# Batch 0 loaded in fp32 over two queues, local v in one transfer per head, and all local masks on Pool, in a sparse-attention and MLP kernel

## The chip, the cores and the metric

The kernel runs on 1 core of one Trainium2 chip. The metric is the device time of one execution in microseconds (us). One look at a kernel gives a profile and a time; where small differences matter it is run several times, in turn with the kernel before on the same chip.

## The reference, cut to what matters

```python
batch, n_heads, seq, head_dim = (8, 8, 576, 64)      # q, k, v: fp32
stride = 32
rel = pos[:, None] - pos[None, :]
mask_local   = (rel >= 0) & (rel < stride)                                  # heads 0..3
mask_strided = (rel >= 0) & (pos[None, :] % stride == pos[:, None] % stride)  # heads 4..7
x = softmax(where(mask, q @ k.T / 8, -1e9)) @ v      # then to [4608, 512]
h = x @ w_in                                         # w_in  [512, 2048]
out = (h * tanh(softplus(h))) @ w_out                # w_out [2048, 512], result fp32
```

## The kernel before

A head loads and computes the attention of batch 0. Then come nine blocks of the MLP, each of 512 tokens: `mlp1` (x to h), then `mlp2` (h to out). The attention of batch t+1 is cut into small steps, which are put between the groups of matmuls of block t. So blocks 0 to 6 carry attention, the last two are MLP alone. "Strided" tiles have 72 partitions, "local" ones 96 or 128.

Loads and casts. Strided k and q are cast from fp32 to bf16 by the transfer itself, which is issued by Pool (GpSimd); everything else of q, k and v comes as fp32 through SP and is cast by an engine. The fp32 buffers `vs32`, `vl32`, `kl32`, `ql32` exist once, so the loads for a later batch wait until the casts of the earlier one are done.

```python
    def load_qk_str(b):
        for dst, src in ((ks, k), (qs, q)):
            nc.gpsimd.dma_start(
                dst[b % 2][0:PN], src[b, 4:8].rearrange("h (p j) d -> p h (j d)", j=CS)
            )
    # ... load_qk_loc: the same for heads 0..3, on nc.sync, into kl32 and ql32 ...

    def load_v(b):
        nc.sync.dma_start(vs32[0:PN], v[b, 4:8].rearrange("h (p j) d -> p h j d", j=CS))
        nc.sync.dma_start(vl32[32:128, 0, :, :], v[b, 0:4, 0:96, :].rearrange("h p d -> p h d"))
        for i in range(1, NW):
            nc.sync.dma_start(
                vl32[:, i, :, :],
                v[b, 0:4, WQ * i - 32:WQ * i + WQ, :].rearrange("h p d -> p h d"),
            )
    # ...
    def cast_v(b, e_s, e_l):
        cast(e_s, vs[b % 2][0:PN, :, :, 0:D], vs32[0:PN])
        for i in range(0, NW, 3):
            cast(e_l, vl[b % 2][:, i:i + 3, :, 0:D], vl32[:, i:i + 3, :, :])
```

The steps of the attention inside a block: `Q` is scores, exponential and mask, with the engine of the mask as its last argument; `V` is P times v and the division by the row sum; `X` transposes to the layout of the MLP.

```python
        return [
            [Q("s", 0, Dv)], [], [Q("s", 1, Dv)],
            [Q("s", 2, Po), V("s", 0)],
            [Q("l", 0, Po), V("s", 1)],
            [Q("l", 1, Po), V("s", 2), V("s", 3)],
            [Q("l", 2, Dv), V("s", 4)], [V("s", 5), V("s", 6)],
            # ... the other V and X steps ...
        ]
```

The head and the main loop:

```python
        load_qk_str(0)
        # ... ident, stm ...
        load_qk_loc(0)
        # ... loc ...
        load_v(0)
        # ... memsets on Dv; transposes of strided k and q ...
        cast_qk_loc(0, Po, Dv)
        cast(Po, vs[0][0:PN, :, :, 0:D], vs32[0:PN])
        load_w_in(0, 2)
        # ... strided scores and masks (Dv); local v cast by Po; load_w_in(2, 4) ...
        # ... local scores and masks (Dv) ...
        for j in range(8):
            a.pv("s", j)
        # ...
        load_qk_loc(1)
        load_v(1)
        # ... the rest of the attention of batch 0 ...
        load_qk_str(1)
        for c in range(4):
            nc.gpsimd.dma_start(w_out[:, 4 * c:4 * c + 4, :], ...)
        cast_qk_loc(1, Po, Po)
        cast_v(1, Po, Po)
        load_qk_str(2)
        # ... load_qk_loc(2), load_v(2) ...
        for t in range(NBLK):
            gT, g1 = mlp1(t)
            # ... mlp1 groups with the transposes of batch t+1 between them ...
            if t + 3 < B:
                load_qk_str(t + 3)
            # ... mlp2 groups with the attention steps of batch t+1 between them ...
            # ... casts of batch t+2 on Po, loads of batch t+3 ...
```

The softmax here doesn't subtract the row's maximum and nothing guards it: scores larger than these inputs give would overflow.

Of the kernel before, what the change touches and what calls it, by code (L numbers as in the profile page):

```python
# [10 lines left out]
F32 = mybir.dt.float32  # L11
BF16 = mybir.dt.bfloat16
AF = mybir.ActivationFunctionType
# [3 lines left out]
NW = 6  # L17
WQ = 96
CL, PL = 6, 96
CS, PN = 8, 72  # L20
# [15 lines left out]
def kernel(ctx, tc, q, k, v, moe_w_in, moe_w_out, out):  # L36
    nc = tc.nc
    B, H, S, D = q.shape
# [8 lines left out]
    loc_h = nc.inline_tensor(loc_np, name="locmask")  # L47
    stm_h = nc.inline_tensor(stm_np, name="strmask")
    ident_h = nc.inline_tensor(
        np.eye(128, dtype=np.float32).astype(ml_dtypes.bfloat16), name="ident"  # L50
    )
# [45 lines left out]
# [5 lines that stand above are left out]
# [5 lines left out]
                src[b, 0:4].rearrange("h (p j) d -> p h (j d)", j=CL),  # L107
            )

    def load_v(b):  # L110
        nc.sync.dma_start(vs32[0:PN], v[b, 4:8].rearrange("h (p j) d -> p h j d", j=CS))
        nc.sync.dma_start(vl32[32:128, 0, :, :], v[b, 0:4, 0:96, :].rearrange("h p d -> p h d"))
        for i in range(1, NW):
            nc.sync.dma_start(
                vl32[:, i, :, :],
                v[b, 0:4, WQ * i - 32:WQ * i + WQ, :].rearrange("h p d -> p h d"),
            )

    def load_w_in(c0, c1):
        for c in range(c0, c1):  # L120
# [5 lines left out]
    def cast(eng, out_, in_):  # L126
        if eng is nc.scalar:
            nc.scalar.copy(out_, in_)  # L128
        else:
            eng.tensor_copy(out_, in_)  # L130

    def cast_qk_loc(b, e_k, e_q):
        for e, dst, src in ((e_k, kl, kl32), (e_q, ql, ql32)):
            cast(e, dst[b % 2][0:PL].rearrange("p j h d -> p h j d"), src[0:PL])
# [131 lines left out]
    def attn_steps(b):  # L266
        a = Attn(b)
        Po, Dv = nc.gpsimd, nc.vector
        Q = lambda kd, i, e: (lambda: a.qk(kd, i, e))
        V = lambda kd, i: (lambda: a.pv(kd, i))  # L270
        X = lambda kd, hf: (lambda: a.xt(kd, hf))
        return [
            [Q("s", 0, Dv)], [], [Q("s", 1, Dv)],
            [Q("s", 2, Po), V("s", 0)],
            [Q("l", 0, Po), V("s", 1)],
            [Q("l", 1, Po), V("s", 2), V("s", 3)],
            [Q("l", 2, Dv), V("s", 4)], [V("s", 5), V("s", 6)],
            [V("s", 7), V("l", 0)], [V("l", 1)], [X("s", 0), V("l", 2)],
            [X("s", 1), V("l", 3)], [X("l", 0), V("l", 4)], [V("l", 5)],
            [X("l", 1)], [],  # L280
        ]
# [48 lines left out]

    with tc.manual_schedule():
        Po, Dv, Sc = nc.gpsimd, nc.vector, nc.scalar
        load_qk_str(0)
        nc.sync.dma_start(ident[:], ident_h.ap())
        nc.sync.dma_start(stm[:], stm_h.ap())
        load_qk_loc(0)
        nc.sync.dma_start(loc[:], loc_h.ap())
        load_v(0)
        Sc.preload_act_table(AF.Exp)
        Dv.memset(kTs[:, 16 * PN:16 * PN + 64], 0.0)  # L340
        Dv.memset(kTl[:, :, 0:32], 0.0)
        Dv.memset(vl32[0:32, 0, :, :], 0.0)
# [3 lines left out]
        for i in range(2):  # L346
            Dv.memset(vl[i][0:32, 0, :, D:D + 1], 0.0)
        for p in P_s + P_l:
            Dv.memset(p[:], 0.0)

        a = Attn(0)
        t_step(0, "s", "k", 0, Dv)
        t_step(0, "s", "k", 1, Dv)
        t_step(0, "s", "q", 0, Sc)
        t_step(0, "s", "q", 1, Sc)
        cast_qk_loc(0, Po, Dv)
        cast(Po, vs[0][0:PN, :, :, 0:D], vs32[0:PN])
        load_w_in(0, 2)
        a.qk("s", 0, Dv)
# [5 lines left out]
        for hp in range(2):  # L365
            t_step(0, "l", "k", hp, Dv)
            t_step(0, "l", "q", hp, Sc)
        a.qk("l", 0, Dv)
        a.qk("l", 1, Dv, True)
        a.qk("l", 2, Dv, True)  # L370
        for j in range(8):
            a.pv("s", j)
        nc.sync.dma_start(gate[:], x_s[0:1, 5, :])
# [77 lines left out]
```

## Time and profile before

| | kernel before |
|---|---|
| median of 3 runs before the prediction | 355.98 us |
| median of the 4 runs beside the changed kernel | 356.06 us (355.93 to 356.62) |
| span of the profiled run, TensorE busy | 354.6 us, 318.3 us |
| first matmul of the MLP | 37.23 us |
| block 0: start of `mlp1(0)` to start of `mlp1(1)` | 37.23 to 75.19 = 37.96 us |
| blocks 1 and 2 | 36.47 and 36.46 us |

"Idle before" in square brackets is the time for which the engine did nothing ahead of that line, and the arrow names what ended it. The lines which the prediction rests on stand in it (timelines: start, duration, engine, line, operation). Two more views matter later. The first is the timeline of Pool in block 0 of the kernel before (start, duration, engine, line, operation):

```profile
53.66 0.83 POOL L130 CAST vl<-vl 128x768 bf16<-128x768 f32 x1 [3.18 <-DMA vl<-in_v_dram]
55.51 0.83 POOL L130 CAST vl<-vl 128x768 bf16<-128x768 f32 x1 [1.02 <-DMA vl<-in_v_dram]
...
60.34 1.27 POOL L211 TENSOR_TENSOR Ps<-Ps,stm 72x576 bf16<-72x576 bf16 x1 [1.19 <-ACT Ps L209]
```

Local v of batch 1 lands by 55.5 us, and the strided mask waits for its exponential on ScalarE, not the reverse: Pool is there in time, with 1.19 us to spare.

The second is the timeline of TensorE's weight loads at the start of the MLP. Each 128x512 matmul has one, so their spacing is the rate of the matmuls:

```profile
40.17 0.15 PEld L301 LDWEIGHTS <-w_in 128*128 128x128 bf16 x1 [0.28 <-issue]
40.60 6.63 PEld L301 LDWEIGHTS <-w_in 128*128 128x128 bf16 x31 [0.27 <-issue]
```

From 37.23 to 40.60 us one comes every 0.43 us; from there on every 0.214 us (6.63 us for 31). The MLP starts at half rate and loses about 1.7 us by it.

### The profile page before, as it was taken

The numbers are of one execution on the slowest core, as the hardware profiler recorded it, in microseconds if no ns is written. First come the engines' busy times: TensorE is split into PE (matmuls) and PEld (weight loads), VectorE is DVE, ScalarE is ACT, GpSimd is POOL, SyncE is SP. The second block draws the span as 40 slices with busy tenths as digits, with TensorE's granted clock in tenths as the row PEclk, the third lists the DMA queues.
The fourth block names the chain that finished last, engine by engine and source line by source line (L and its number), as shares of the span: only waits on it lengthen the run. The fifth ranks groups of instructions, "written<-read, shape, count | busy, mean of one in ns | idle before, by whom it ended". The sixth has DMA issues, their size and how long they took to land.

```text
span 354.6 us, 6492 instructions
## 1 busy us (share of the span) xinstructions
PE 318.3 (90%) x2784; PEld 171.2 (48%) x2784; DVE 124.9 (35%) x327; ACT 173.6 (49%) x190; POOL 100.6 (28%) x88
## 2 busy tenths in 40 slices
PE   0537999899989998999899989998999989999994
PEld 0424454455445544554469745554555454444441
DVE  3478025632363236323642364235613460000000
ACT  1431556275636564556446653666275636514611
POOL 3290236911091109310841065005600400000000
PEclk9999999999999999999999999999999999999999
DMA  7999999969611991099109901870110011011012
GB/s 172 187 163 211 265 187 213 179 167 233 108 61 59 217 139 59 20 246 148 48 15 238 172 4 61 207 139 1 61 61 0 3 61 59 0 61 59 0 44 76
DMA packets 49073, 39.03 MB, mean 110 GB/s; under 512 B 27284, under 2 KB 42132, under 8 KB 49044
## 3 DMA queue, kind: packets, MB, share of 16 engines
q1 hardware_dynamic: 38420, 29.70, 36.1%
q0 software_dynamic: 10624, 8.92, 16.2%
q8 instruction: 22, 0.36, 0.5%
q14 instruction: 7, 0.06, 0.1%
HBM read 38.08 MB, written 9.44 MB: 134 GB/s over the span
## 4 chain that ended last, share of the span: by engine, by line
PE 79%; DVE 8%; ACT 6%; DMA 3%; issue 3%; POOL 0%; ACTq 0%; POOLq 0%
PE psh L301 36%; PE pso L316 29%; PE po L227 4%; DMA qs<-in_q_dram 3%; PE tr L150 2%; PE tr L159 2%; ACT Pl L209 2%; DVE Pl L211 2%; PE ps L191 2%; ACT Ps L209 2%; DVE x_s L234 2%; PE ps L202 2%; DVE Ps L211 1%; DVE qTl L130 1%; PE trx L257 1%
## 5 line engine op out<-in xcount | busy, mean ns | idle before, releaser
L316 PE MATMUL pso<-w_out,gT 128*128 128x512 bf16 x576 | 141.5, 379 | 0.0
L301 PE MATMUL psh<-xT,w_in 128*128 128x512 bf16 (+1 forms) x640 | 135.3, 361 | 0.8 <-ACT xT L128 0.7
L305 ACT ACTIVATE gT<-psh 128x1024 bf16<-128x1024 f32 x72 | 73.8, 1024 | 55.9 <-PE psh L301 55.7
L301 PEld LDWEIGHTS <-w_in 128*128 128x128 bf16 x640 | 60.3, 99 | 55.3 <-issue 3.4
L316 PEld LDWEIGHTS <-gT 128*128 128x128 bf16 x576 | 49.0, 97 | 44.3
L128 ACT COPY xT<-trx 128x576 bf16<-128x576 bf16 x32 | 20.4, 639 | 55.4 <-PE trx L257 39.5
L211 POOL TENSOR_TENSOR Ps<-Ps,stm 72x576 bf16<-72x576 bf16 x7 | 8.9, 1269 | 101.4 <-ACT Ps L209 101.4
L323 ACT COPY osb<-pso 128x1024 f32<-128x1024 f32 x18 | 18.2, 1012 | 27.8 <-PE pso L316 27.8
L233 DVE RECIPROCAL rden<-po 72x4 f32<-72x4 f32 (+1 forms) x112 | 19.7, 176 | 29.6 <-PE po L227 29.6
L227 PE MATMUL po<-vs,Ps 72*128 72x65 bf16 x256 | 18.2, 201 | 11.8 <-DVE rden L233 8.7
L234 DVE TENSOR_TENSOR x_s<-po,rden 72x256 bf16<-72x256 f32 x64 | 26.9, 420 | 2.2
L209 ACT ACTIVATE Pl<-ps 128x768 bf16<-128x768 f32 x24 | 19.2, 811 | 13.8 <-PE ps L191 13.8
L130 DVE COPY kTs<-tr 128x576 bf16<-128x576 bf16 x16 | 7.3, 458 | 47.6 <-PE tr L150 47.5
L211 POOL TENSOR_TENSOR Pl<-Pl,loc 128x768 bf16<-128x768 bf16 x14 | 22.6, 1639 | 1.9 <-ACT Pl L209 1.9
L209 ACT ACTIVATE Ps<-ps 72x864 bf16<-72x864 f32 (+1 forms) x24 | 19.1, 806 | 7.1 <-PE ps L202 7.0
L211 DVE TENSOR_TENSOR Ps<-Ps,stm 72x864 bf16<-72x864 bf16 (+1 forms) x17 | 14.0, 831 | 23.5 <-ACT Ps L209 23.5
L227 PEld LDWEIGHTS <-Ps 72*128 72x128 bf16 x256 | 12.6, 101 | 18.9 <-issue 9.4
L234 DVE TENSOR_TENSOR x_l<-po,rden 96x256 bf16<-96x256 f32 x48 | 20.2, 420 | 1.7
L130 DVE COPY kTl<-tr 128x576 bf16<-128x576 bf16 x16 | 12.0, 756 | 18.8 <-PE tr L159 18.8
L130 POOL CAST kl<-kl 96x1536 bf16<-96x1536 f32 x8 | 13.7, 1707 | 17.3 <-DMA kl<-in_k_dram 17.3
L130 POOL CAST vs<-vs 72x2048 bf16<-72x2048 f32 x8 | 15.1, 1893 | 10.5 <-DMA vs<-in_v_dram 10.5
L99 POOL DMA_DIRECT2D ks<-in_k_dram x8 | 6.2, 779 | 36.8 <-PE tr L150 36.0
(44 smaller groups left out, 223.0 us busy)
## 6 DMA issues: line engine op xcount, KB each, us to landing
out_dram<-osb SPq DMA_DIRECT2D x18, 512.0 KB, 2.8
vl<-in_v_dram SPq DMA_DIRECT2D x40, 128.0 KB, 12.2
kl<-in_k_dram SPq DMA_DIRECT2D x8, 576.0 KB, 5.5
ql<-in_q_dram SPq DMA_DIRECT2D x8, 576.0 KB, 7.8
vs<-in_v_dram SPq DMA_DIRECT2D x8, 576.0 KB
ks<-in_k_dram POOLq DMA_DIRECT2D x8, 288.0 KB, 10.9
qs<-in_q_dram POOLq DMA_DIRECT2D x8, 288.0 KB, 11.1
w_in<-in_moe_w_in_dram POOLq DMA_DIRECT2D x4, 512.0 KB, 7.5
```

The source lines that it names most:

```text
L128: nc.scalar.copy(out_, in_)
L130: eng.tensor_copy(out_, in_)
L150: nc.tensor.transpose(tr[:, PN * u:PN * u + PN], src[0:PN, h, 128 * jj:128 * jj + 128], ident[0:PN, 0:PN],)
L209: nc.scalar.activation(pt[0:n, :, 0:nw], ps[0:n, :, 0:nw], AF.Exp, scale=scale)
L211: meng.tensor_tensor(out=pm, in0=pm, in1=mk[0:n, :].unsqueeze(1).unsqueeze(1).to_broadcast([n, 2, nu, w]), op=ALU.mult,)
L227: nc.tensor.matmul(po[:, h, :], lhsT=pt[0:n, c0:c0 + 128], rhs=rhs, start=True, stop=True,)
L233: nc.vector.reciprocal(rden[0:m, :], po[0:m, :, D])
L234: nc.vector.tensor_tensor(out=dst.rearrange("p (h d) -> p h d", h=4), in0=po[0:m, :, 0:D], in1=rden[0:m, :].unsqueeze(2).to_broadcast([m, ...
L301: nc.tensor.matmul(ps[:, u, o:o + n], lhsT=w_in[:, cc, fc * 128:(fc + 1) * 128], rhs=xT[:, cc, a:a + n], start=(cc == 0), stop=(cc == 3),)
L305: nc.scalar.activation(gT[:, 2 * g:2 * g + 2, :], ps[:], AF.Mish)
L316: nc.tensor.matmul(p[:, ot % 2, :], lhsT=gT[:, fc, 128 * ot:128 * ot + 128], rhs=w_out[:, fc, :], start=(fc == 0), stop=(fc == 15),)
L323: nc.scalar.copy(osb[:], p[:])
```

## The change

The intent: start the attention of batch 0 earlier, by loading its strided k and q first, in fp32, through SP into the still unused buffers of the MLP, and the local v beside them through ScalarE's queue; fewer transfers for local v; VectorE relieved of the local masks.

```diff
-    def load_v(b):
+    def load_v(b, eng=None):
         nc.sync.dma_start(vs32[0:PN], v[b, 4:8].rearrange("h (p j) d -> p h j d", j=CS))
-        nc.sync.dma_start(vl32[32:128, 0, :, :], ...)
-        for i in range(1, NW):
-            nc.sync.dma_start(vl32[:, i, :, :], ...)
+        eng = eng or nc.sync
+        eng.dma_start(vl32[32:128, 0, :, :], ...)
+        for h in range(4):
+            win = bass.AP(v.tensor, v[b, h:h + 1, WQ - 32:WQ, :].offset,
+                          [[D, 128], [WQ * D, NW - 1], [1, D]])
+            eng.dma_start(vl32[:, 1:NW, h, :], win)
@@ the steps of a block
-            [Q("l", 2, Dv), V("s", 4)], [V("s", 5), V("s", 6)],
+            [Q("l", 2, Po), V("s", 4)], [V("s", 5), V("s", 6)],
@@ the head
-        load_qk_str(0)
-        nc.sync.dma_start(ident[:], ident_h.ap())
-        nc.sync.dma_start(stm[:], stm_h.ap())
+        Sc.preload_act_table(AF.Exp)
+        st0 = []
+        for src in (k, q):
+            st = g_pool.tile([128, 16, 512], BF16, tag="gT", name="st0")
+            ... # seen as fp32, 72 x 2048
+            nc.sync.dma_start(st..., src[0, 4:8].rearrange("h (p j) d -> p h (j d)", j=CS))
+            st0.append(st)
+        Sc.dma_start(ident[:], ident_h.ap())
+        Sc.dma_start(stm[:], stm_h.ap())
+        Sc.dma_start(loc[:], loc_h.ap())
         load_qk_loc(0)
-        nc.sync.dma_start(loc[:], loc_h.ap())
-        load_v(0)
+        load_v(0, Sc)
@@
-            Dv.memset(p[:], 0.0)
+            Po.memset(p[:], 0.0)
+        cast(Dv, ks[0]..., st0[0])
+        cast(Sc, qs[0]..., st0[1])
@@
-        cast_qk_loc(0, Po, Dv)
+        cast_qk_loc(0, Dv, Dv)
@@
-        a.qk("l", 0, Dv)
-        a.qk("l", 1, Dv, True)
-        a.qk("l", 2, Dv, True)
+        a.qk("l", 0, Po)
+        a.qk("l", 1, Po, True)
+        a.qk("l", 2, Po, True)
```

More of the change, by code (lines that the diff above doesn't have):

```diff
@@ L108, in load_qk_loc @@
             )
-    def load_v(b):
+    def load_v(b, eng=None):
         nc.sync.dma_start(vs32[0:PN], v[b, 4:8].rearrange("h (p j) d -> p h j d", j=CS))
-        nc.sync.dma_start(vl32[32:128, 0, :, :], v[b, 0:4, 0:96, :].rearrange("h p d -> p h d"))
-        for i in range(1, NW):
-            nc.sync.dma_start(
-                vl32[:, i, :, :],
-                v[b, 0:4, WQ * i - 32:WQ * i + WQ, :].rearrange("h p d -> p h d"),
+        eng = eng or nc.sync
+        eng.dma_start(vl32[32:128, 0, :, :], v[b, 0:4, 0:96, :].rearrange("h p d -> p h d"))
+        for h in range(4):
+            win = bass.AP(
+                v.tensor, v[b, h:h + 1, WQ - 32:WQ, :].offset, [[D, 128], [WQ * D, NW - 1], [1, D]]
             )
+            eng.dma_start(vl32[:, 1:NW, h, :], win)
     def load_w_in(c0, c1):
@@ L332 @@
         Po, Dv, Sc = nc.gpsimd, nc.vector, nc.scalar
-        load_qk_str(0)
-        nc.sync.dma_start(ident[:], ident_h.ap())
-        nc.sync.dma_start(stm[:], stm_h.ap())
+        Sc.preload_act_table(AF.Exp)
+        st0 = []
+        for src in (k, q):
+            st = g_pool.tile([128, 16, 512], BF16, tag="gT", name="st0")
+            st = st[:].rearrange("p a b -> p (a b)").bitcast(F32)[0:PN, 0:4 * CS * D]
+            nc.sync.dma_start(
+                st.rearrange("p (h x) -> p h x", h=4),
+                src[0, 4:8].rearrange("h (p j) d -> p h (j d)", j=CS),
+            )
+            st0.append(st)
+        Sc.dma_start(ident[:], ident_h.ap())
+        Sc.dma_start(stm[:], stm_h.ap())
+        Sc.dma_start(loc[:], loc_h.ap())
         load_qk_loc(0)
-        nc.sync.dma_start(loc[:], loc_h.ap())
-        load_v(0)
-        Sc.preload_act_table(AF.Exp)
+        load_v(0, Sc)
         Dv.memset(kTs[:, 16 * PN:16 * PN + 64], 0.0)
@@ L348 @@
         for p in P_s + P_l:
-            Dv.memset(p[:], 0.0)
+            Po.memset(p[:], 0.0)
         a = Attn(0)
+        cast(Dv, ks[0][0:PN].rearrange("p h x -> p (h x)"), st0[0])
+        cast(Sc, qs[0][0:PN].rearrange("p h x -> p (h x)"), st0[1])
         t_step(0, "s", "k", 0, Dv)
```

## The prediction

> **What bounds the kernel now.** I read the page's first part and its slices, then the chain of work that ended last, then the waits, and then the timeline engine by engine for the first 38 us and for one block in the middle. TensorE is busy 318.3 of 354.6 us at full granted clock, so at most about 36 us is to be had, and the question is where those 36 us lie.
>
> ```profile
> PE   0537999899989998999899989998999989999994
> PEclk9999999999999999999999999999999999999999
> DMA  7999999969611991099109901870110011011012
> PE 79%; DVE 8%; ACT 6%; DMA 3%; issue 3%; POOL 0%; ACTq 0%; POOLq 0%
> ```
>
> Each digit of the first three lines is a slice of 8.9 us. TensorE is idle or thin in the first four slices and never again. This head holds nearly all the idle time: the first matmul of the MLP starts at 37.23 us. The first dip after the head is the one below, and it comes back in every block.
>
> ```profile
> PE po L227 <- DVE rden L233: 7.5, 6, 1.3
> 101.08 0.89 DVE L211 TENSOR_TENSOR Pl<-Pl,loc 128x768 bf16<-128x768 bf16 x1 [0.93 <-ACT Pl L209]
> 101.90 0.17 DVE L233 RECIPROCAL rden<-po 72x4 f32<-72x4 f32 x1
> 102.10 0.42 DVE L234 TENSOR_TENSOR x_s<-po,rden 72x256 bf16<-72x256 f32 x1
> 102.67 0.28 PE L227 MATMUL po<-vs,Ps 72*128 72x65 bf16 x4 [1.25 <-DVE rden L233]
> ```
>
> The first line is from the waits between 75 and 294 us: six waits, 7.5 us. The others are the timeline of one of these blocks. VectorE sits behind the third local mask, which waits for its exponential (0.93 us) and runs 0.89 us; the normalization of the fifth strided tile queues behind it, so its PSUM buffer comes free late, and TensorE stands 1.25 us. The seventh such wait is in the first block (1.19 us). Sum 8.7 us, the figure that the page gives for L227 behind rden. Otherwise the blocks run back to back: one lasts 111.66 - 75.19 = 36.47 us.
>
> The head, from the timelines of the engines:
>
> ```profile
> 8.53 1.14 PE L150 MATMUL tr<-ident_sb,ks 72*128 72x72 bf16 x16 [8.53 <-DMA ks<-in_k_dram]
> 12.33 1.14 PE L150 MATMUL tr<-ident_sb,qs 72*128 72x72 bf16 x16 [2.66 <-DMA qs<-in_q_dram]
> 15.49 1.90 POOL L130 CAST vs<-vs 72x2048 bf16<-72x2048 f32 x1 [7.20 <-DMA vs<-in_v_dram]
> 17.33 1.53 POOL L121 DMA_DIRECT2D w_in<-in_moe_w_in_dram  x2
> 15.64 5.52 DVE L211 TENSOR_TENSOR Ps<-Ps,stm 72x864 bf16<-72x864 bf16 x3 [3.11 <-ACT Ps L209]
> 21.08 1.41 DVE L130 COPY kTl<-tr 128x576 bf16<-128x576 bf16 x2
> 24.46 1.96 DVE L211 TENSOR_TENSOR Pl<-Pl,loc 128x768 bf16<-128x768 bf16 x3 [1.97 <-ACT Pl L209]
> ```
>
> Strided q lands at 12.3 us; the three strided masks take 5.5 us of VectorE while Pool casts v and issues weight loads (the same 72x864 mask takes 0.60 us in a later block); the local half follows on the same engine, and 14 normalizations fill VectorE from 26.34 to 35.79 us.
>
> **What the Trainium skill says.** "DMA: Bandwidth & Descriptors", section "Issuing engines are not separate DMA queues", says that transfers from any engine interleave on the same 16 DMA engines and that another issuer saves only issue time. The trace agrees as far as it goes: with loads from SP and Pool under way, the DMA share is over 1 from 4 to 16 us and the rate only 190 to 260 GB/s. So I gain from order and descriptor kind, not from the second queue. "SBUF — State Buffer", section "SBUF: two separate sides", calls the port pair of VectorE and Pool an exclusive lock against a two-input VectorE operation. The trace agrees: 0.60 us alone, up to 2.57 us for one beside a Pool cast. "GPSIMD Engine Reference", section "4.1 Engine selection", puts two-input elementwise work on Pool at about twice VectorE's time; here the 128x768 mask is 1.64 us on Pool against 0.79 us mean on VectorE.
>
> **The change, part by part.**
>
> *All local masks on Pool, in blocks 0 to 6.* VectorE loses a wait and 0.89 us at the point where TensorE waits; Pool gets a third mask of 1.64 us, and starts its casts for a later batch that much later. In the block shown Pool finishes the second mask at about 101.5 us, so the third ends near 103.2; its reader, the local PV of the fifth window, runs at 107.3 us. That is off the path by 4 us. The Pool casts end at 108 us and would end at 109.7; the load that overwrites their source is issued only at 113.4 us. How much of the 1.25 us comes back: a PV to the end of its normalization takes about 0.96 us, and the next normalization 0.54 us more. Without the mask the normalization of strided tile 6 would end near 102.63 us, while TensorE would want its buffer at 102.4; with 0.15 us of signalling, 0.4 us stays. So 0.85 us a block, at best 1.25: 7 x 0.85 = 6.0 us, at best 8.7. I take 6.5.
>
> *Strided k and q of batch 0 in fp32 through SP.* They go first in the queue, as 2 KB rows that the hardware queue moves at 380 to 400 GB/s when alone (the output stores in the middle of the trace: 0.52 MB in about 1.4 us). 0.59 MB is 1.55 us each. Issued at 0.75 us, first bytes about 1 us later (as for ident): estimated landing 4.2 us for k and about 6 us for q. Price: two casts of 72x2048, about 1.2 us on VectorE (0.96 us for 96x1536 scaled) and 1.9 us on ScalarE (0.81 us for 768 columns, 1.01 us for 1024). ScalarE must first issue five loads of local v, 2944 runs of 256 B. In the kernel before SP stood up to 3.75 us in one such issue once some 2000 runs were outstanding; I expect ScalarE to be held until about 8 us. So cast 8 to 9.9, transposes and copies to about 11, first exponential near 11.5 us against 14.72: 3 us earlier.
>
> *Local k and q.* Their casts move to VectorE ahead of the strided masks (about 1 us each). With about 12 us of transfer for the head (five loads of 0.59 MB at 1.55 us, 0.75 MB of local v at the 187 GB/s seen from 15.5 to 18.5 us) local q should land near 11 and strided v near 13.5 us (before: 15.49). The masks then run about 12.5 to 15.8 us instead of 15.64 to 21.1, mostly before Pool's cast of v takes the port pair.
>
> *Local v, one transfer per head.* The same 2560 runs of 256 B in four issues instead of five. I give it nothing.
>
> *Memsets to Pool.* About 5 us of Pool before it has other work: free.
>
> *Where the head ends now.* Two chains. VectorE: masks to 15.8, two kTl copies 1.4, normalizations 9.5 (as before), then 1.44 us from the last normalization to the first MLP matmul (37.23 - 35.79): about 28.1 us. Pool: from the landing of v, 1.9 cast + 1.5 issue + 2.0 casts of local v + 1.5 issue + three masks of 1.64 = 11.8 us, then 1.65 us for the last two PV and normalizations and 1.44: 13.5 + 14.9 = 28.4 us. I take 29 us for slips, 8.2 us earlier than 37.23.
>
> *Given back.* The weights and batch 1 still have to come: from 17 us on 7.3 MB by destination at 205 to 260 GB/s last to about 50 us in both kernels, and the loads of w_out are issued behind the masks on Pool (at about 26 instead of 23.7 us). With an MLP that starts 8 us earlier, the transposes of batch 1 want their k at 39 us and mlp2 its weights at 46.5. I estimate k landed at 36 to 38 and w_out at 43 to 48: tight, 1 us lost.
>
> Sum: 355.98 - 6.5 - 8.2 + 1.0 = 342.3 us; I say 342.5.
>
> **The rivals.** (1) The stall in the blocks only moves: Pool's third mask, or the next normalization, holds the PV instead. For it: VectorE does 0.54 us a tile and TensorE asks nearly as fast. Against it: 4 us of slack at the reader. Then about 349 us. (2) The head is bound by DMA, so an earlier start is paid back as waits for weights or batch 1 in the first block. For it: the DMA share of 9 in slices 1 to 8. Against: those waits are absent now, with 5 us or more of slack for batch 1's strided k. Then 346 to 347 us. (3) ScalarE is stuck in its DMA issues until 12 us or more, and the head gains only 3 to 4 us: about 347 us. (4) All goes well, the whole 8.7 us and 9 us come back: 338 us.
>
> **Range and chances.** Rivals 1, 2 and 3 each leave a gain over 2% or close to it (349 us); only two together fall short of it. Nothing in the change adds work on TensorE, and the path it touches has slack. Range 338 to 348 us; faster by over 2% 0.90, within 2% 0.09, slower 0.01.
>
> **What would show it.** In the changed profile: strided q landed by 6 us and the ScalarE cast of it beginning near 8; first strided mask before 13 us and each near 0.6 us; first MLP matmul at 28 to 30 us; no TensorE wait over 0.5 us for rden in blocks 1 to 6, and blocks of about 35.6 us. I am wrong if the three Pool masks in the head begin later than 22 us, if the first block is longer than 38 us through waits for ks, w_out or vs, or if a PV waits for Pool in each block.

## More of the kernel before

Pool works in program order. In block 0 its list is therefore: the casts of batch 1 as its data land, last the local v; four issues of strided k and q (batches 2 and 3); then the mask of the third strided tile and the local masks of block 0.

## The result, and the profile after

The changed kernel takes 355.47 us in the median of 4 runs (354.36 to 355.58), the kernel before 356.06 us beside it. The ratio is 0.9973, with a 95% interval of 0.9951 to 0.9996: the same, where I had said 342.5. A ratio here and below is the mean time of one kernel's runs over that of the other's of the same rounds, so not quite the ratio of the medians that are quoted. Executions over 1.5% slower than the fastest of the same kernel are left out of the means. Its profile is of the fastest of the four runs, with a span of 352.6 us, 2.0 us under that of before.

| us | before | after | difference |
|---|---|---|---|
| first matmul of the MLP | 37.23 | 36.32 | -0.9 |
| block 0 | 37.96 | 43.05 | +5.1 |
| blocks 1 to 6, each | 36.46 | 35.45 | 6 x -1.0 |

So one part came as forecast, one hardly at all, and block 0 took back most of the rest. First the page of the changed kernel: two of the lines by slices, and the chain of work that ended last.

```profile
PE   1355899599999999999999999999999999999994
PEclk9999999789999999999999999999999999999998
PE 71%; issue 8%; POOL 5%; DMA 5%; SPq 4%; DVE 3%; ACT 3%; POOLq 0%; ACTq 0%
```

The idle slices at the start are still there. A new dip stands in the eighth slice (62 to 70 us), with the granted clock (the share of TensorE's full clock that the throttle let through) down beside it, and the chain now has DMA, SP's queue and Pool with 14% together where before it had 3% of DMA.

**The blocks.** The waits of TensorE between 75 and 294 us, in the changed kernel:

```profile
PE po L228 <- DVE rden L234: 1.5, 6, 0.2
```

Six waits of 1.3 us have become six of 0.2 us. This is the part that worked.

**The head.** The timelines of VectorE and ScalarE give the landings, since each cast starts when its data are there:

```profile
6.33 1.22 DVE L131 CAST ks<-st 72x2048 bf16<-72x2048 f32 x1 [4.49 <-DMA st<-in_k_dram]
...
17.98 0.95 DVE L131 CAST ql<-ql 96x1536 bf16<-96x1536 f32 x1 [2.64 <-DMA ql<-in_q_dram]
18.86 1.49 DVE L212 TENSOR_TENSOR Ps<-Ps,stm 72x864 bf16<-72x864 bf16 x3
```

```profile
2.96 6.56 ACTq L118 DMA_DIRECT2D vl<-in_v_dram  x4
9.83 1.90 ACT L129 CAST qs<-st 72x2048 bf16<-72x2048 f32 x1 [7.81 <-DMA st<-in_q_dram]
```

Strided k was there at 6.3 us and q at 9.8 us (forecast 4.2 and 6), local q at 18.0 (forecast 11). The three strided masks take 0.5 us each instead of 1.84, as forecast, but they stand in VectorE's order behind the cast of local q and start at 18.9 us, not 12.5 (15.64 in the kernel before). ScalarE was held in its four issues until 9.5 us, a little longer than the forecast 8.

The waits of SP's queue in the first 15 us (what it waited for; total, times, longest):

```profile
SPq L105 <- DMA loc<-locmask: 4.6, 1, 4.6
SPq L105 <- DMA ident_sb<-ident: 3.2, 1, 3.2
```

SP held back the issues of local k and q until small loads on ScalarE's queue had landed, although no data require it. What makes it wait is not shown: in m3 below the same loads stand in the same order up to strided v, and SP issues local k and q at 1.64 and 2.09 us. Here local q was issued at 9.73 us. And the stretches of 2 us (last three columns: granted clock, share of the DMA engines, GB/s) show the rate:

```profile
14.00:16.00 2.00, 1.34 (x31) 1.01 (x25) 0.96 (x1) 1.76 (x3) 0.00 (x0) 1.00 0.87 200
16.00:18.00 2.00, 0.06 (x1) 0.00 (x0) 0.02 (x1) 0.44 (x1) 0.00 (x0) 1.00 0.82 204
...
22.00:24.00 2.00, 1.54 (x28) 1.23 (x27) 0.18 (x2) 1.51 (x3) 2.00 (x3) 1.00 0.04 8
```

The loads move at 200 GB/s with the DMA engines over 80% busy, half of the rate that I had taken from the output stores. Five loads of 0.59 MB and 0.75 MB of local v are 3.7 MB, and they were done when strided v landed at 20.84 us: 3.7 MB in the 19.3 us since about 1.5 us is 192 GB/s. After that the DMA stands still until Pool, which casts v first, issues the weights.

**Block 0.** The timeline of Pool in the changed kernel:

```profile
20.84 1.89 POOL L131 CAST vs<-vs 72x2048 bf16<-72x2048 f32 x1 [15.31 <-DMA vs<-in_v_dram]
22.67 1.71 POOL L122 DMA_DIRECT2D w_in<-in_moe_w_in_dram  x2
...
61.75 1.60 POOL L131 CAST vl<-vl 128x768 bf16<-128x768 f32 x2 [14.70 <-DMA vl<-in_v_dram]
63.30 0.75 POOL L99 DMA_DIRECT2D ks<-in_k_dram  x1
...
66.17 1.28 POOL L212 TENSOR_TENSOR Ps<-Ps,stm 72x576 bf16<-72x576 bf16 x1
```

Local v of batch 1 lands at 61.75 us, 6.2 us later than before; the first weights too were issued 5.3 us later (17.33 before). Pool stands idle for 14.7 us in wait for it, then casts, then does four issues, and only then the mask that TensorE waits for. The timeline of TensorE at that point:

```profile
67.51 0.40 PE L228 MATMUL po<-vs,Ps 72*128 72x65 bf16 x4 [3.65 <-POOL Ps L212]
67.72 1.90 PE L317 MATMUL pso<-w_out,gT 128*128 128x512 bf16 x4
```

and in stretches of 2 us (the clock is the third figure from the right):

```profile
68.00:70.00 2.00, 2.00 (x13) 1.04 (x12) 0.67 (x3) 0.00 (x0) 2.00 (x2) 0.50 1.38 169
70.00:72.00 2.00, 2.00 (x11) 0.83 (x9) 0.99 (x4) 0.00 (x0) 2.00 (x2) 0.50 1.36 160
```

TensorE pauses 3.65 us, and after the pause its clock is granted at half until about 73 us: four matmuls take 1.90 us instead of 1.03. That is 3.65 us and, as an estimate, half of some 5.4 us more, 2.7 us. The Trainium skill, "TensorE: Matmul & The Clock Gate", section "What's actually happening", says that after an idle window of some 3.4 us the array falls to half rate, and that as much busy time lifts it again. The trace agrees with the fall, after 3.65 us; the half rate then lasted some 5.4 us. So this was to be had in advance, once a pause was expected.

Why does local v land so late? Packets of the DMA queues in the changed kernel from 48 to 54 us (packets, MB, share of the engines):

```profile
q0 software_dynamic: 943, 0.94, 91.7%
q1 hardware_dynamic: 949, 0.24, 30.0%
```

q0 is Pool's queue, here w_out; q1 is SP's, here rows of local v, 256 B each. The engines take packets from the two queues one for one, and as a packet of w_out is four times as large, w_out gets four fifths of the bytes. "DMA: Bandwidth & Descriptors", section "Queues, rings and completion order", says that each DMA engine goes round the queues by packets; the equal counts agree. So local v crawls until w_out is done, and its end follows the sum of the traffic since the weights began: local v of batch 1 had landed 38.2 us after the first issue of w_in in the kernel before, and 39.1 us after it in the changed one. By that landing the DMA engines had moved 10.96 MB in the kernel before and 11.85 MB in the changed one; 0.59 MB of the difference is strided k and q of batch 0, which now arrive in fp32 and not in bf16. And from 20 to 24 us they moved 4 GB/s, since the weights were issued only at 22.67 us.

### The profile page after: what moved, and what is told of

It is laid out like the page before. It is cut to its first block, busy times and chain, and to the rows that moved or that the text cites. A ratio compares the mean times of both kernels' runs of the same rounds, so it can differ in the third digit from the quotient of the medians.

```text
span 352.6 us, 6444 instructions
## 1 busy us (share of the span) xinstructions
PE 317.1 (90%) x2737; PEld 172.1 (49%) x2784; DVE 113.9 (32%) x313; ACT 175.6 (50%) x191; POOL 115.9 (33%) x101
## 2 busy tenths in 40 slices
DMA packets 48745, 39.62 MB, mean 112 GB/s; under 512 B 26956, under 2 KB 41228, under 8 KB 48716
## 4 chain that ended last, share of the span: by engine, by line
PE 71%; issue 8%; POOL 5%; DMA 5%; SPq 4%; DVE 3%; ACT 3%; POOLq 0%; ACTq 0%
PE psh L302 31%; PE pso L317 28%; DMA vl<-in_v_dram 5%; PE po L228 4%; SPq L118 4%; PE tr L151 2%; PE tr L160 2%; ACT Ps L210 2%; DVE x_s L235 1%; PE ps L192 1%; POOL Pl L212 1%; DVE qTl L131 1%; PE ps L203 1%; PE trx L258 1%; PE trx L248 1%
## 5 line engine op out<-in xcount | busy, mean ns | idle before, releaser
L317 PE MATMUL pso<-w_out,gT 128*128 128x512 bf16 x546 | 139.5, 384 | 1.6 <-issue 0.2
L302 PE MATMUL psh<-xT,w_in 128*128 128x512 bf16 (+1 forms) x623 | 133.7, 359 | 1.8 <-ACT xT L129 0.7
L212 POOL TENSOR_TENSOR Pl<-Pl,loc 128x768 bf16<-128x768 bf16 x24 | 38.6, 1637 | 1.7 <-ACT Pl L210 1.6
L228 PE MATMUL po<-vs,Ps 72*128 72x65 bf16 x256 | 17.5, 203 | 5.0 <-POOL Ps L212 3.6
L131 POOL CAST vs<-vs 72x2048 bf16<-72x2048 f32 x8 | 15.2, 1896 | 18.9 <-DMA vs<-in_v_dram 18.9
L131 POOL CAST vl<-vl 128x768 bf16<-128x768 f32 x16 | 12.8, 832 | 18.3 <-DMA vl<-in_v_dram 18.3
L228 PE MATMUL po<-vl,Pl 128*128 128x65 bf16 x192 | 14.6, 202 | 4.5 <-POOL Pl L212 2.5
L131 DVE COPY kTl<-tr 128x576 bf16<-128x576 bf16 x16 | 12.1, 757 | 18.9 <-PE tr L160 18.8
L212 DVE TENSOR_TENSOR Ps<-Ps,stm 72x864 bf16<-72x864 bf16 (+1 forms) x17 | 10.0, 595 | 20.3 <-ACT Ps L210 20.3
## 6 DMA issues: line engine op xcount, KB each, us to landing
vl<-in_v_dram SPq DMA_DIRECT2D x28, 160.0 KB, 13.5
```

What stands on the lines that cost most here:

```text
L131: eng.tensor_copy(out_, in_)
L212: meng.tensor_tensor(out=pm, in0=pm, in1=mk[0:n, :].unsqueeze(1).unsqueeze(1).to_broadcast([n, 2, nu, w]), op=ALU.mult,)
L228: nc.tensor.matmul(po[:, h, :], lhsT=pt[0:n, c0:c0 + 128], rhs=rhs, start=True, stop=True,)
L302: nc.tensor.matmul(ps[:, u, o:o + n], lhsT=w_in[:, cc, fc * 128:(fc + 1) * 128], rhs=xT[:, cc, a:a + n], start=(cc == 0), stop=(cc == 3),)
L317: nc.tensor.matmul(p[:, ot % 2, :], lhsT=gT[:, fc, 128 * ot:128 * ot + 128], rhs=w_out[:, fc, :], start=(fc == 0), stop=(fc == 15),)
```

## The experiments

Theory after the result: (1) the masks in the blocks are worth 6 us; (2) the head gained little since the transfers are slower than I took them, and local v through ScalarE's queue competes with strided v; (3) block 0 lost because traffic brings local v of batch 1, Pool with it, and the mask late; a pause then costs more than its length, through the clock. Rivals are named in each expectation. "Head" is the start of the first MLP matmul.

### One part alone

**m1.** The kernel before, with the third local mask of each block on Pool.

```diff
-            [Q("l", 2, Dv), V("s", 4)], ...
+            [Q("l", 2, Po), V("s", 4)], ...
```

> The kernel before with one word changed: the third local mask of blocks 0 to 6 on Pool, nothing else. Theory A (the masks in the blocks are worth about 1 us each, and block 0 lost them in the changed kernel only because its loads came late): all seven blocks gain, 7 x 1.0 = 7 us, so 349 us (348 to 350), blocks of 35.45 us, head unchanged at 37.2 us, no TensorE wait for Pool in block 0. Rival (block 0's stall in the changed kernel is made by the longer row of Pool masks itself): block 0 stalls here too, and the gain stays under 5 us: 351 us or more.

350.24 us (349.24 to 351.05; kernel before 356.22), ratio 0.9823 [0.9796, 0.9851]. Blocks 35.46 us, no wait for Pool in block 0, head 37.15. One changed word gives 6 us; the rest of the change takes 5 of them away.

**m2.** The changed kernel, with that mask back on VectorE.

> The changed kernel with the third mask of the blocks put back on VectorE: new head, old blocks. Theory A: head 0.9 us earlier, block 0 about 5 us longer or a little more, blocks of 36.45 us: 355.5 + 6 = 361 us (359.5 to 362.5), slower than before. Rival (head changes are neutral, the steady gain was smaller than the trace seems to show): 355 to 357 us.

360.43 us, ratio 1.0112 [1.0086, 1.0137]. Head 36.96, block 0 43.3 us with the pause (3.75 us) and the clock at 0.50, later blocks 36.45. The two parts add up to within some 1 us: the rest of the change alone is a loss of 4 us.

**m3.** The changed kernel, local v of batch 0 on SP, behind strided v.

```diff
-        load_v(0, Sc)
+        load_v(0)
```

> The changed kernel with the local v of batch 0 behind the other loads on SP instead of on ScalarE's queue. Theory A (local v takes its share of the DMA engines ahead of need and, through the waits of the kl and ql issues for earlier loads, holds back local k and q and strided v): strided q lands by 8 us (9.73), strided v by 17 us (20.84), w_in is issued by 19.5 us (22.67), the first MLP matmul comes at 33.5 us or earlier (36.32), block 0 is shorter than 41 us; total about 350 us. Rival (the DMA engines are full anyway, so the order of the head loads moves nothing): head within 1 us of 36.3, total 354 to 356 us.

350.90 us, ratio 0.9846 [0.9821, 0.9872]. Strided v lands at 18.02 instead of 20.84 us, w_in is issued at 19.85, the head ends at 33.52, and local v of batch 1 lands at 59.21. The timeline of Pool in m3:

```profile
18.02 1.89 POOL L131 CAST vs<-vs 72x2048 bf16<-72x2048 f32 x1 [12.48 <-DMA vs<-in_v_dram]
...
59.21 1.60 POOL L131 CAST vl<-vl 128x768 bf16<-128x768 f32 x2 [14.87 <-DMA vl<-in_v_dram]
```

The second queue cost 4.6 us. It brought no bandwidth (217 GB/s from 2 to 18 us in the changed kernel, 212 in m3), and it put local v, which is wanted late, beside strided v, which is wanted early. Two things changed at once here: SP's waits of 3.2 and 4.6 us were gone too, and m3 doesn't part them from the competition. Strided q did not come by 8 us as forecast, but at 10.18.

**m4.** The changed kernel, the first weights issued ahead of Pool's cast of strided v.

```diff
-        cast(Po, vs[0][0:PN, :, :, 0:D], vs32[0:PN])
         load_w_in(0, 2)
+        cast(Po, vs[0][0:PN, :, :, 0:D], vs32[0:PN])
```

> The changed kernel with the issue of the first two w_in loads ahead of the cast of strided v on Pool. Theory A (the loads of block 0 end late because w_in is issued only when strided v has landed, with the DMA engines idle from 20.5 to 23 us): the batch 1 loads end 2 to 4 us earlier, block 0 stalls less for Pool, but the head ends later by up to 3 us because w_in now competes with its loads; sum 352 to 356 us. Rival (block 0's stall comes from the per-head transfers of local v, not from when w_in starts): block 0's Pool wait stays over 3 us.

354.75 us, ratio 0.9951. The head moved to 37.88 (the cast of v ran at 24.08), local v landed at 62.77, wait 2.99 us. The time fits the theory's range, but local v did not come earlier, and the wait is next to the rival's 3 us. The profile says why: the gap in the traffic was moved and not closed, for Pool now stood 16.9 us in wait ahead of the second pair of weights, and from 24 to 28 us the DMA engines moved nothing.

**m5.** The kernel before, with only local v in one transfer per head, on SP.

```diff
-        for i in range(1, NW):
-            nc.sync.dma_start(vl32[:, i, :, :], ...)
+        for h in range(4):
+            win = bass.AP(...)            # as in the change
+            nc.sync.dma_start(vl32[:, 1:NW, h, :], win)
```

> The kernel before with local v in one transfer per head in every batch, nothing else. Theory A (the number of 256 B rows sets the cost, not how they are cut into transfers): within 1 us of before, local v of batch 1 landed by 54.5 us, as before. Rival (the per-head transfers make local v of batch 1 land late and stall block 0): local v of batch 1 landed after 57 us, block 0 at least 2 us longer, total 358 us or more.

360.65 us, ratio 1.0113 [1.0089, 1.0136]: the part that I gave nothing costs 4 us by itself, although the head is 2 us earlier (35.17). A cast takes three windows of all four heads. By windows the first half could be cast at 53.66 us, while the second half was still on the way; by heads both wait for the last head, 56.30 us. Pool is then late with its masks, VectorE's own third mask runs beside them, and in the timeline of VectorE in m5 it takes 4.33 us instead of 0.89:

```profile
62.98 4.33 DVE L211 TENSOR_TENSOR Pl<-Pl,loc 128x768 bf16<-128x768 bf16 x1 [0.94 <-ACT Pl L209]
```

TensorE paused 4.69 us and fell to the clock of 0.50. The rival said that local v would land after 57 us; it did not, so its result held and its mechanism only in part. The exclusive port pair, which the prediction cites, would explain the 4.33 us: the mask ran beside two Pool masks and a Pool cast (62.26 to 66.84 us). No run takes that apart from Pool's lateness, which was only 0.7 us at the strided mask (61.03 against 60.34).

### Pool's order and its masks

**m6.** The changed kernel, with the issues of strided k and q of batch 1 and of w_out ahead of Pool's masks in the head.

```diff
+        load_qk_str(1)
+        for c in range(4): nc.gpsimd.dma_start(w_out[...], ...)
         a.qk("l", 0, Po)
         # ... and taken away from behind the head
```

> The changed kernel with the loads of ks, qs of batch 1 and w_out issued on Pool before its three local masks of the head instead of after them. Theory A (while both queues have packets the DMA engines take them in turn one for one, so 256 B rows of local v crawl as long as w_out is under way; w_out issued late means local v of batch 1 late): with w_out issued 4.8 us earlier local v of batch 1 lands by 58.5 us (61.6), the Pool wait of block 0 falls from 3.65 to about 1 us, and its half-clock stretch shortens; the head ends later by about 3 us, since the masks start 4.5 us later. Sum 352 to 355 us. Rival (w_out has nothing to do with it): Pool wait of block 0 stays over 3 us and the total rises to 358 us.

353.63 us, ratio 0.9926. Local v landed at 61.63, not by 58.5: earlier issues of w_out do not bring it earlier, as the traffic is the same. The head ended at 41.37, as TensorE waited 6.9 us for Pool's masks there; in block 0 it no longer waited for Pool, and the clock stayed at 1.00. The wait was moved, not removed.

**m7.** The changed kernel, head masks on VectorE.

```diff
-        a.qk("l", 0, Po) ...
+        a.qk("l", 0, Dv) ...
```

> The changed kernel with the three local masks of the head back on VectorE; those of the blocks stay on Pool. Theory A: Pool issues ks, qs and w_out 4.8 us earlier without a price on VectorE above 1 us; local v of batch 1 lands by 58 us, Pool wait of block 0 under 1.5 us, head at 36 to 37 us; total 351 to 353 us. Rival (the head is bound by Pool's masks, and they must stay off VectorE): head later than 38 us, total 355 us or more.

355.03 us (352.98 to 356.38), ratio 0.9953: missed, and where the rival had it (head later than 38 us, total 355 or more). Head 38.64, local v 63.58, pause 2.8 us.

**m8.** m3 and m7 together.

> The changed kernel with both mends: local v of batch 0 on SP behind the other loads, and the local masks of the head on VectorE. Theory A (the two losses are separate and add): head at about 34 us, local v of batch 1 landed by 55 us, no Pool wait in block 0 over 0.5 us, no half-clock stretch, total 347 us (345.5 to 348.5), better than the masks alone on the kernel before (350.2 us). Rival (DMA-bound up to 60 us whatever the order): 350 us or more.

351.92 us, ratio 0.9871, against 347: missed, and no better than m3 alone. Head 35.27, pause 2.2 us. Pool's masks in the head are not what costs time; I withdrew that suspicion.

**m11.** The changed kernel, with strided k and q of batch 2 issued before the casts of local v, those of batch 3 after the masks of block 0.

```diff
-        cast_v(1, Po, Po)
-        load_qk_str(2)
+        cast(Po, vs[1]..., vs32[0:PN])
+        load_qk_str(2)
+        ... cast local v ...           # load_qk_str(3) follows the attention of block 0
```

> The changed kernel with only the order of Pool's DMA issues around block 0 altered: ks and qs of batch 2 issued before the casts of batch 1's local v, those of batch 3 after block 0's masks, so that 2.9 us of issues no longer stand between the landing of local v and the strided mask. Theory B: local v lands at 61.7 us as before, the strided mask starts at 63.3 instead of 66.2 us, TensorE's wait falls from 3.65 to about 0.8 us, the half-clock stretch goes; total about 351 us (350 to 352.5). Rival (Pool's late mask is not what holds TensorE): 355 us.

353.92 us, ratio 0.992: missed. Taking 2.9 us of issues out of Pool's way helped by 1.5 us at most (the intervals touch), for the earlier issue put more traffic ahead of local v (12.49 MB moved by its landing against 11.85), which landed at 66.80 us, 5 us later; pause 3.3 us. This first pointed at the amount of traffic.

### Local v by windows again

**m10.** The changed kernel with the transfers of local v by windows.

> The changed kernel with local v by windows again in all batches, batch 0's still on ScalarE's queue. Theory B: first cast of batch 1's local v 36 us after the w_in issue, near 58.5 us instead of 61.75, so the wait for Pool in block 0 falls from 3.65 to about 1 to 1.5 us and the half-clock stretch goes; total 351.5 us (350.5 to 352.5). Rival: the lateness is all from w_in, the cut makes no difference: 355 us.

353.38 us (352.06 to 354.59), ratio 0.9902. Casts at 54.72 and 62.58 us; the second half lands as late as by heads, but it alone is left to cast. Pause 1.93 us, and the clock stays at 1.00. Worth some 2 us, less than forecast; the two intervals only just miss each other.

**m9.** m10 with local v on SP, as in m3.

> The changed kernel with local v by windows again (all batches) and that of batch 0 on SP behind the other loads. Theory B (from strided v's landing a chain runs to block 0: cast on Pool, issue of w_in, then some 36 us of full DMA engines until the first windows of batch 1's local v are there, 39 us until all heads are; then Pool's casts, four DMA issues, and the strided mask that TensorE waits for): w_in issued near 19.9 us, first cast of batch 1's local v at 55.7 us, strided mask of block 0 on Pool by 61 us, TensorE wait of about 0.3 us in place of 2.7 (vl on SP, per head), total 347 us (346 to 348.5). Rival (the cut into windows or heads does not matter inside the changed kernel): 350.9 us as with heads on SP.

349.84 us (348.40 to 351.16), ratio 0.9816 [0.9787, 0.9845]. Head 33.09, casts at 50.80 and 58.87, pause 1.7 us (forecast 0.3), clock 1.00. It is 3 us short of the forecast, and only level with m1, although its head ends 4 us earlier than that of m1. This question was left for m18 and m19.

### The suspected causes by themselves

**m12.** m1, with Pool repeating its strided mask of block 3 five times more: a pause made on purpose (the mask is 0 and 1, so the result stays right).

```diff
+            for _ in range(6 if (self.b, kind, i) == (4, "s", 2) else 1):
                 meng.tensor_tensor(out=pm, in0=pm, in1=mk..., op=ALU.mult)
```

> The kernel with block masks on Pool only (350.2 us), with Pool repeating its strided mask of block 3 five times more (same result), so that TensorE must wait about 3 us there, far from any shortage of DMA. Theory C (a TensorE pause of over 2 us in the middle of the MLP halves the granted clock for some 4 to 6 us afterwards): granted clock near 0.5 after the pause, and the total rises by about 3.2 + 2.5 = 5.7 us to 356 us. Rival (the half clock in block 0 has to do with block 0 or the DMA load): full clock, total rises by the pause alone, to 353.5 us.

355.20 us, ratio 0.9957, 5.0 us over m1. The timeline of TensorE in m12:

```profile
174.44 0.40 PE L228 MATMUL po<-vs,Ps 72*128 72x65 bf16 x4 [3.44 <-POOL Ps L212]
174.65 1.90 PE L317 MATMUL pso<-w_out,gT 128*128 128x512 bf16 x4
```

The clock was at 0.50 from 174 to 180 us and back at 0.99 from there. Block 3 of m12 lasts 41.3 us in the profile, that of m1 35.4: a pause of 3.44 us costs 5.9, some 2.4 of it through the clock. (The medians differ by less, 5.0 us; the start at half rate of m12 was 1.7 us shorter in its profile, worth 0.85.) So that a pause by itself brings the half clock is shown, with no shortage of DMA in it.

**m15.** The changed kernel with a quarter of w_out loaded and the rest set to zero: 1.57 MB less traffic. Its output is wrong, which doesn't matter for the time.

```diff
-        for c in range(4):      # loads of w_out
+        for c in range(1):
+        Dv.memset(w_out[:, 4:16, :], 0.0)
```

> The changed kernel with only the first quarter of w_out loaded and the rest set to zero on VectorE at the start (a wrong result on purpose), which takes 1.57 MB of bf16, about 7.5 us of DMA time, out of the first 60 us. Theory B (amount of traffic): batch 1's local v lands near 54.5 us instead of 61.7, TensorE does not wait for Pool in block 0, the clock stays full, total 349.5 us (348.5 to 351). Rival (local v waits for its turn in its own queue whatever else runs): landed after 59 us, a pause of over 2 us, total 353 us or more.

349.00 us, ratio 0.9791 [0.9771, 0.9811]. The timeline of Pool in m15:

```profile
52.99 1.60 POOL L131 CAST vl<-vl 128x768 bf16<-128x768 f32 x2 [5.79 <-DMA vl<-in_v_dram]
...
59.42 1.27 POOL L212 TENSOR_TENSOR Ps<-Ps,stm 72x576 bf16<-72x576 bf16 x1 [2.05 <-ACT Ps L210]
```

Local v lands 8.8 us earlier, Pool waits for the exponential again, TensorE does not wait for Pool, the clock stays at 1.00. With the head unchanged (36.44), 6.5 us are back. So the loss in block 0 hangs on the traffic ahead of local v, shown by taking it away. What it doesn't show is that the change added this traffic: w_out is as large in the kernel before. There the traffic began 5.3 us earlier and was 0.9 MB less.

**m14.** m3, with the 72-partition loads of batch 0 cut into 64 and 8 partitions, to test whether the slow loads use too few DMA engines.

```diff
-            nc.sync.dma_start(st..., src[0, 4:8]...)
+            for p0, p1 in ((0, 64), (64, PN)):
+                nc.sync.dma_start(st...[p0:p1], src[0, 4:8]...[p0:p1])
```

> The changed kernel with local v of batch 0 on SP (350.9 us with whole loads), and the three strided loads of batch 0 each cut in 64 + 8 partitions. Theory D (a 72-partition load[...] took 3.1 to 3.5 us where a 96-partition load of the same bytes took 2.35 us[...]): strided q landed by 8.5 us (10.18), strided v by 15.8 us (18.02), w_in issued by 17.6 us, first MLP matmul near 31.5 us, total 348.5 us. Rival (the time is set by the rows' size and count, or by more transfers waiting for one another): landings within 0.7 us of the whole loads, total 350.9 us.

353.30 us, ratio 0.9908, 2.4 us worse than m3. q landed at 10.65 (10.18 in m3) and strided v at 20.06 (18.02). The theory fell; why the cut costs time is not shown.

**m16.** The changed kernel, strided k and q of batch 0 cast by Pool's transfer as in the kernel before.

```diff
-        for src in (k, q): ...            # fp32 into the g buffers, and the two casts
+        load_qk_str(0)
```

> The changed kernel with strided k and q of batch 0 loaded as before (cast in the DMA, issued by Pool first of all), no staging and no casts of them; all else as changed. Theory E (the fp32 loads cost the DMA engines about 3 us more than the casting ones, and this delays strided v, w_in and all that follows): strided v landed by 18 us (20.84), w_in issued by 19.8 us (22.67), local v of batch 1 by 59 us, total 352.5 us (351 to 354). Rival (the lateness comes from local v on ScalarE's queue and the waits for earlier loads alone): strided v landed at 20 us or later, total 355 us or more.

351.46 us, ratio 0.986. Strided v at 16.08, w_in at 17.92, as expected; local v of batch 1 at 60.78, almost 43 us after w_in, so the 37 to 40 us of most runs are no constant.

**m17.** m16 with local v by windows and on SP.

> As the run without fp32 loads, and also local v by windows on SP behind the other loads: what is left of the change is the masks on Pool, the memsets on Pool and the casts of local k and q on VectorE. Theory E: strided v landed near 16 us, w_in issued near 18 us, local v of batch 1 by 56.5 us, head at 33 to 34 us, no pause over 2 us, total 348 us (346.5 to 349.5), the best so far. Rival (the masks of the head on Pool hold the head back whatever the loads do): head at 36 us or later, total 350 us or more.

349.92 us (349.20 to 351.77), ratio 0.9823: missed by 2 us. Strided v at 14.12 us, but the head ends at 35.64, and not at 33 to 34. No pause was left in block 0, as forecast; its start at half rate lasted 5.9 us.

The four kernels together give the landing of strided v: 20.84 us as changed, 18.02 with local v on SP, 16.08 without the fp32 staging, 14.12 with neither. So the second queue costs it 2 to 3 us, the staging 4 to 5. The staging brought strided k 4 us earlier (6.33 against 10.4 in m16), and with m16 and m17 the strided masks start only at 19.0 and 19.5 us, for want of strided q. It moves the wait from one tile to another, and the transfers do not grow less by it: the pages count 39.62 MB moved in the changed kernel and 39.03 MB in the kernel before.

### The start of the MLP

**m18.** m9 with nine matmuls of 128x512 into a buffer that is not read, in the pauses of TensorE before the MLP.

```diff
+        def warm(n):
+            for _ in range(n):
+                nc.tensor.matmul(wps[:, 0, :], lhsT=ident[:], rhs=kTs[:, 0:512], start=True, stop=True)
+        warm(3)
         a.pv("l", 0); a.pv("l", 1)
+        warm(2)
         a.pv("l", 2); a.xt("s", 0); a.xt("s", 1); a.pv("l", 3)
+        warm(1)
         a.pv("l", 4); a.pv("l", 5)
+        warm(1)
         a.xt("l", 0); a.xt("l", 1)
+        warm(2)
```

> m9 (windows restored, local v on SP) with nine extra matmuls of 128x512 on data that is already there, placed in the pauses of TensorE between 24 and 34 us; their result is never read. Theory: the first matmuls of the MLP run at half rate (one every 0.43 us from 33.5 to 39.0 in m9, 3 us lost) because TensorE is too thinly used before them. With the fillers the half-rate stretch after the first MLP matmul is shorter than 3 us, and the total is 347.5 to 348.8 us (m9: 349.84). Rival: the stretch depends on something else or on chance; it stays over 4.5 us and the total is 349.8 to 350.5.

351.38 us (349.94 to 352.20), ratio 0.9859 [0.9838, 0.9880]: missed; 1.5 us more than m9 in the median, with intervals that still touch, and surely no gain. Yet the stretch at half rate was gone: 5.9 us (33.09 to 39.02) in m9, 0.3 us (33.96 to 34.28) in m18. TensorE got to the mask earlier, the mask did not: local v landed at 59.20 (58.87 in m9). The pause grew from 1.73 to 2.73 us, and that was enough for the clock to fall to 0.50 between 66 and 68 us; 1.1 us of wait for strided q of batch 1 came on top. An earlier MLP is not worth anything here until local v comes earlier.

**m19.** m1 with the same nine matmuls.

> m1 (kernel before with the third local mask of the blocks on Pool) with the same nine fillers. Theory: half-rate stretch of 4.6 us in m1 shrinks to under 2.5, total 348.5 to 349.7 (m1: 350.24). Rival: stretch unchanged, total 350.2 to 351.

348.36 us (347.87 to 348.97), ratio 0.9776 [0.9762, 0.9791]: a little under the forecast, and the best of all versions. The timelines of the weight loads, first m1, then m19:

```profile
41.37 0.15 PEld L301 LDWEIGHTS <-w_in 128*128 128x128 bf16 x1 [0.28 <-issue]
41.79 5.97 PEld L301 LDWEIGHTS <-w_in 128*128 128x128 bf16 x28 [0.28 <-issue]
```

```profile
38.02 0.10 PEld L301 LDWEIGHTS <-w_in 128*128 128x128 bf16 x1 [0.36 <-issue]
38.41 8.09 PEld L301 LDWEIGHTS <-w_in 128*128 128x128 bf16 x38 [0.28 <-issue]
```

m1 runs at half rate from 37.15 to 41.79 us; m19 starts 0.9 us later and is at full rate from 38.41 on. Its block 0 lasts 35.50 us, as long as the others. So the half rate comes from the thin use of TensorE in the head, and where nothing behind it is short, its 2 us can be had. m19 is the kernel before with one mask moved and nine unread matmuls: 2.2% faster than the kernel before, and 7 us faster than the changed one.

## Why the prediction was wrong

**All local masks on Pool (-6.5 us): right.** Forecast 0.85 to 1.25 us a block; measured 1.0 in each of blocks 1 to 6, the 1.2 us wait of block 0 gone as well, and 6 us for m1. Rival 1 did not come about: the slack of the mask's reader was 4.4 us in block 1, as worked out.

**The head (-8.2 us): wrong, -0.9 us.** The failed step is "0.59 MB is 1.55 us each". The rate was that of output stores; these loads ran at 200 GB/s, although the prediction itself quotes 190 to 260 GB/s for the loads of the head. All landings that follow from it were late: local q at 18.0 instead of 11, strided v at 20.84 instead of 13.5. The formula behind it held: landing plus 14.9 us forecast, plus 15.5 measured. So did the shorter masks on VectorE and, nearly, ScalarE's hold. A second step was missing: local v on ScalarE's queue competes with strided v, though the prediction itself had quoted that another queue brings no bandwidth (m3: 2.8 us of landing and of head). A third is that SP waited for the small loads on ScalarE's queue, which the order of instructions did not show; in m3 that went too, so the 2.8 us are for both together.

**"I give it nothing" for local v per head: wrong.** It costs 4 us alone (m5) and about 2 us inside the change (m10). I counted runs of 256 B and not what the casts wait for.

**Given back (1.0 us): wrong, about 6.3 us.** I looked at w_out and strided k of batch 1. What came late was local v of batch 1, which nothing on TensorE reads at that time; but Pool's cast of it stands ahead of a mask that TensorE does read. The pause is 3.65 us, and the clock after it about 2.7 us. m15 shows that the pause hangs on the traffic ahead of local v, and m12 that a pause brings the half clock. Rival 2 named the kind, "paid back as waits in the first block", yet it had the wrong waits; its 346 to 347 us mean some 5 us given back in all, near the 6.3 measured.

The sum from the profiles: blocks 1 to 6 -6.0, block 0's own wait -1.2, head -0.9, start at half rate -0.2 (2.9 us of it instead of 3.4), pause and clock +6.3: -2.0 us, the difference of the two spans. This is the fastest run of the changed kernel; the medians differ by 0.6 us.

Three readings of the prediction are off, and none decided it: the longest strided mask beside a Pool cast took 3.15 us, not 2.57; 187 GB/s fits 14.5 to 17.5 us (188), while 15.5 to 18.5 us has 129, as the transfers end in it; and the DMA digit is not 9 in all of slices 1 to 8 (the first is 7).

Left open: why the fp32 loads run at 200 GB/s (cutting them into 64 and 8 partitions did not help, m14; the number of partitions was not varied by itself, though in m3 a 96-partition load landed 2.3 to 2.4 us after the load before it and a 72-partition load of the same bytes 3.1 to 3.5 us); why local v follows w_in by 37 us in one kernel and 43 in another; and how much of the scatter of 1 to 2 us between similar kernels is the length of the half-rate start, which went from 2.8 to 5.9 us in the profiles of kernels without fillers.

## What to carry to other kernels

Before you count an earlier start as a gain, find what else has to arrive by a fixed amount of traffic, and follow every in-order engine that waits for it to the first thing TensorE wants from that engine: here a load that nobody needed yet held a mask. Take transfer rates from the same kind of transfer in the same stage, loads from loads. And try each part of a change alone; one moved mask, with a TensorE kept busy up to the first large matmul, was worth more than the rest.

## What the Trainium skill lacked or had wrong

- "TensorE: Matmul & The Clock Gate", section "Why this matters for your kernels", warns of pauses over about 3 us. Here 2.20 us (m8), 2.39 us (m16) and 2.66 us (m3) were already followed by a clock of 0.50 to 0.56 over 2 us; 1.73 us (m9) and 1.93 us (m10) were not.
- The same page, section "What's actually happening", puts the cost of a start at half rate under 1% of a typical span, and advises against fitting a count to it. Here it was of that size, but to be had: filler matmuls in the pauses before removed it (4.6 us of half rate in m1, 0.4 us in m19: 1.9 us of the total, 0.5%). The profile's granted clock read 1.00 in such a stretch (36 to 42 us in m17, a weight load every 0.43 us), so it has to be read from the spacing.
- "SBUF — State Buffer", section "Door 1: The DMA port swizzle", lists rates by number of partitions, but none for 72 or 96. Here fp32 loads into these ran at 200 GB/s with a DMA share of 0.82 to 0.87, while output stores of 0.52 MB passed in about 1.4 us.
- "DMA: Bandwidth & Descriptors" has the turns by packets, but no page that I read says what they mean for two queues with unequal rows: equal counts of packets (943 and 949 in 6 us) gave the queue with 256 B rows 0.24 MB and the other 0.94 MB.
